# Block-sparse attention and a GELU feed-forward on one core: the first unit's last sampled values moved by SyncE's DMA instead of GpSimd's copies, weights and keys asked for earlier, five more idle products, and new orders for the later units

## The chip, the cores and the metric

The kernel runs on one core of one Trainium2 chip. The metric is the device time in microseconds of one execution; the median of three runs stands for a kernel. PE is TensorE, DVE is VectorE, ACT is ScalarE, POOL is GpSimd and SP is SyncE, as in the profile.

## The reference, cut to what matters

```python
B, H, S, D = 4, 8, 768, 64        # q, k, v in float32
block, n_blocks, n_rand = 32, 24, 3
scores = q @ k^T / sqrt(D)
# a query block sees: itself and its two neighbours, block 0, block 23,
# and its 3 sampled blocks; the query blocks 0 and 23 see everything
attn = softmax(where(mask, scores, -1e9)) @ v
x = attn.transpose(0, 2, 1, 3).reshape(B * S, H * D)      # 3072 x 512
h = x @ w_in                                              # 512 x 2048
out = (0.5 * h * (1 + erf(h / sqrt(2)))) @ w_out          # 2048 x 512
```

The numbers of the sampled blocks are an input, so which blocks are fetched is known only on the device.

## The kernel before

The 24 query blocks of each of the four batches are worked off in two units, so there are eight units in all. The first unit of a batch holds the two query blocks that see everything (the dense rounds, in the plan's letters group d) and three groups a, b and c of block rows, up to four query blocks each; the second holds three groups. Units are numbered from one here; the array `units` counts from 0, and `PLANS[1]` to `PLANS[7]` belong to units two to eight.

Every query block with a window sees eight key blocks. The sampled three are put side by side in the tile `gb`: one copy per block and sampled number, whose source position is a register that holds the block's number (`gather`, line 299). A copy of the keys has 128 columns, one of the values 260, one of both 388. The tiles `kv0` and `kv1` hold keys and values of the even and the odd batches; for the first batch the keys lie in `k0`.

A unit goes through two phases. In its attention phase, scores (line 346), a maximum on DVE (372, 375), exponentials on ACT (389, 393), a transpose on DVE (406, 411), products with the values (433, 470), a division on DVE (485 to 489) and a transpose and copy of the result into `xT` (499, 507, 512) follow one another for every round. PE fills the gaps with FFN2 products of the unit before (`ffn2_pieces`, line 566). Then comes FFN1, 64 products of 128x384 with a GELU behind every two output tiles (523, 545).

The order on every engine is the order of the program: a plan, written as a string of words, is read from left to right. `s3` is the score of round 3, `m3` its maximum, `e3` its exponentials, `t3` its transpose; `wa`, `da`, `oa` are the value products, division and output of group a (`wd0` and `wd1` two halves, `Oc` the output in two parts); `f5` takes five products from the filler; `S` stores finished rows, `G` loads the GELU table; a word that starts with `x` calls a function by name. In the first unit the filler is not FFN2 but `idle_products` (line 572): 128x128 by 128x512 products of the identity matrix, whose result nobody reads. In unit two `xk0`, `xq0` and so on turn the second batch's keys and queries, a pair of heads at a time (`turn_pair`, line 246); a `d` at the end gives the copy behind it to DVE, otherwise ACT makes it.

In the first unit most of the sampled blocks are copied by POOL. Its queue, in order: the loads of the first batch, the first half of `w_in` (lines 666 and 669), the keys of groups b and c, and then, called by the plan as `xv0`, `xv1`, `xv2`, the values of groups a, b and c (`values_of`, line 674). Between them it asks for the last two quarters of `w_in` and, after group c's values, for `w_out` in two halves and the second batch's keys and queries in four transfers (lines 685 to 689). All of these transfers convert from float32 to bf16 and stand in one queue. A group's value products read their sampled values from `gb`:

```python
src = sampled(unit.place[j], c - 4)[:, c0:c0 + V2]
...
work.append((s, 1, c, src))
```

At the end of the first unit the plan reads `... t9 db xn wc ob xa dc xb Oc xc`: `xa`, `xb` and `xc` are FFN1 products of the columns that are ready by then. SP issues one small load at the start and then only the stores of the output, and from the third batch on the transposes by DMA.

The tile `g` (128 x 16 x 384, bf16) takes the GELU's result in FFN1 and is read by FFN2 in the next unit.

Of the kernel before, what the change touches and what calls it, by code (L numbers as in the profile page):

```python
# [20 lines left out]
def kernel(  # L21
# [80 lines left out]
    def sampled(i, r):  # L102
        c0 = GW * (i // 3) + 4 * BW + DW * (i % 3) + BW * r
        return gb[:, c0:c0 + BW]

    def keys(b):
        return kvs[b % 2][:, :, 0:KC]
# [311 lines left out]
    def values(unit, grp, halves):  # L419
# [6 lines left out]
        if grp[0][0] == "d":  # L426
            pv = ptd.rearrange("p g c x q e -> p g c (x q) e")
            for c in range(NB // 2 * halves[0], NB // 2 * (halves[-1] + 1)):
                for G in range(2):
                    for h in range(2):  # L430
                        rows = slice(64 * h, 64 * h + 64)
                        c0 = KC + V2 * G
                        nc.tensor.matmul(av[64 * G:64 * G + 64, h, 0:V2],  # L433
                                         lhsT=pv[rows, G, c // 2, :, c % 2],
                                         rhs=kv[rows, c, c0:c0 + V2],
                                         start=(c == 0), stop=(c == NB - 1))
            n, m = 4, 2
        else:
            slots = [j for rnd in grp for j in rnd[1]]
            pv = st[grp, "pt"].rearrange("p g c (q e) -> p g c q e", e=2)  # L440

            shared = len(slots) == 4
            for G in halves:
                c0 = KC + V2 * G
                ends = [(0, 4, c, kv[:, blk, c0:c0 + V2]) for c, blk in ((0, 0), (7, NB - 1))] if shared else []
                work = []
                for c in range(1, 7) if shared else range(8):
                    for s, j in enumerate(slots):
                        if c in (0, 7):
                            blk = 0 if c == 0 else NB - 1  # L450
                            if abs(blk - j) <= 1:
                                continue
                            src = kv[:, blk, c0:c0 + V2]
                        elif c < 4:
                            src = kv[:, j - 2 + c, c0:c0 + V2]
                        else:
                            src = sampled(unit.place[j], c - 4)[:, c0:c0 + V2]
                        work.append((s, 1, c, src))
                work = work + ends if len(halves) == 2 and G else ends + work
                fresh, left = set(range(len(slots))), {s: 0 for s in range(len(slots))}  # L460
                for s, w, _, _ in work:
                    for x in range(s, s + w):
                        left[x] += 1
                for s, w, c, src in work:
                    at = range(s, s + w)
                    for x in at:
                        left[x] -= 1
                    for h in range(2):
                        rows = slice(64 * h, 64 * h + 64)
                        nc.tensor.matmul(av[32 * s:32 * (s + w), h, V2 * G:V2 * G + V2],  # L470
                                         lhsT=pv[rows, G, c % 4, BL * s:BL * (s + w), c // 4], rhs=src[rows],
                                         start=s in fresh, stop=left[s] == 0)
                    fresh -= set(at)
            n, m = len(slots), 4
            if 1 in halves:
                st.pop((grp, "pt"))
# [95 lines left out]
    def idle_products(m):  # L572

        op = psO.tile([P, D_MODEL], F32, name="op", tag="op")
        for _ in range(m):
            nc.tensor.matmul(op, lhsT=identity, rhs=qT0[:, 0].rearrange("p r s -> p (r s)"),
                             start=True, stop=True)
            yield

    def store_finished():  # L580
# [90 lines left out]
    gather(units[0], grps[2], others, 0, KC, nc.gpsimd)  # L671
    others |= block_numbers(grps[0], POOL)

    def values_of(t):

        def ask():
            js = grps[t]
            if t != 1:
                i = 2 - t // 2
                gather(units[0], js[:i], others, KC, BW, nc.gpsimd)  # L680
                load_w_in(2 + t // 2)
                js = js[i:]
            gather(units[0], js, others, KC, BW, nc.gpsimd)
            if t == 2:
                load_w_out(0, 2)
                load_w_out(1, 2)
                for hs in HALVES:
# [5 lines left out]
    def more_numbers(js):  # L693
        def load():
            for c in range(0, len(js), 6):
                known.update(block_numbers(js[c:c + 6], DVE))
        return load
    attention(units[0], idle_products(21),
# [3 lines left out]
              {"f1": lambda: fixed(1), "f2": lambda: fixed(2, nc.scalar.copy, 0),  # L702
               "f3": lambda: fixed(2, nc.scalar.copy, 1), "v0": values_of(0), "v1": values_of(1),
               "v2": values_of(2), "n": more_numbers(J1[:3]),
               "a": lambda: ffn1_ahead(0, (0, 0, P), (0, 1, P)),
               "b": lambda: ffn1_ahead(0, (0, 0, 2 * P)),
               "c": lambda: ffn1_ahead(0, (0, 1, 2 * P), (2, 0, 2 * P), (2, 1, 2 * P))})
# [1 line left out]
    def next_keys(b):  # L709
# [1 line left out]
        spare_key(keys(b))  # L711

    PLANS = {
# [17 lines left out]
    }  # L731

    for n, unit in enumerate(units):
# [83 lines left out]
```

## Time and profile before

| | us |
|---|---|
| median of 3 runs | 273.88 |
| lowest and highest run | 273.58, 276.53 |
| the profiled execution, all of it | 275.15 |
| its span, first to last instruction | 273.4 |
| PE busy in the span | 250.3 |
| mean granted clock of PE | 0.988 |

The span ends 1.75 us short of the profiled execution's time; what lies around it is not in the trace. The page gives, for the whole span, busy time by engine, forty equal slices of 6.8 us (a digit is a tenth), the queues, and groups of instructions by source line. The windows give the same for any stretch, and the timeline gives the instructions of one engine with the idle time before each and what ended it. Ends of PE's products are modelled, and a few records can be missing.

### The profile page before, as it was taken

To read this page: it belongs to the slowest core of one execution; us is meant where nothing else is said; L and a number is where in the kernel's file an instruction comes from. 1 tells how busy PE (TensorE), PEld (TensorE's weight loads), DVE (VectorE), ACT (ScalarE), POOL (GpSimd) and SP (SyncE) were. 2 spreads that over 40 slices of the span, in tenths; PEclk is the share of its full clock that TensorE was granted. 3 is DMA by queue.
4 is the path that set the end of the run, shared out by engine and by line. 5 is a ranking of instruction groups with operands and counts; after the bars stand their busy time and mean duration, and the time that the engine had idled before them with its cause. 6 is when DMAs were issued, how large, how long until landed. Compare 5 with 4: busy or idle time off the path is not lost.

```text
span 273.4 us, 11478 instructions
## 1 busy us (share of the span) xinstructions
PE 250.3 (92%) x4899; PEld 143.7 (53%) x4933; DVE 208.3 (76%) x477; ACT 206.7 (76%) x378; POOL 101.7 (37%) x210
## 2 busy tenths in 40 slices
PE   0798699899999999999999999999999999999995
PEld 0624486355564555545555566455645655465544
DVE  7599969598898989589998987698949996882000
ACT  8679766896868885797868976988788966985611
POOL 7797980717595000950962003910040033000000
PEclk9999689999999999999999999999999999999999
DMA  6999499959999317991997108991101110111002
GB/s 96 183 70 163 75 148 193 206 116 122 63 161 142 102 43 112 114 88 42 120 152 119 62 35 154 89 61 44 40 0 43 43 41 0 38 44 43 0 38 77
DMA packets 73508, 23.80 MB, mean 87 GB/s; under 512 B 63089, under 2 KB 70514, under 8 KB 73458
## 3 DMA queue, kind: packets, MB, share of 16 engines
q0 software_dynamic: 57440, 13.64, 84.4%
q1 hardware_dynamic: 16018, 9.44, 13.6%
q8 instruction: 38, 0.62, 1.0%
q14 instruction: 12, 0.10, 0.1%
HBM read 27.26 MB, written 6.29 MB: 123 GB/s over the span
## 4 chain that ended last, share of the span: by engine, by line
PE 73%; DMA 9%; ACT 6%; DVE 5%; issue 3%; POOL 3%; POOLq 0%; ACTq 0%
PE hp L523 27%; PE op L566 22%; PE av L470 9%; PE sc L346 6%; DMA kn<-in_k_dram 6%; DMA qn<-in_q_dram 3%; PE tx L499 2%; PE op L596 2%; ACT L417 2%; PE pt L234 2%; PE av L433 2%; ACT pp L393 2%; PE av L596 1%; POOL gb L304 1%; ACT pp L389 1%
## 5 line engine op out<-in xcount | busy, mean ns | idle before, releaser
L523 PE MATMUL hp<-xT,w_in_sb 128*128 128x384 bf16 (+2 forms) x536 | 84.9, 319 | 0.2 <-ACT xT L507 0.2
L389 ACT ACTIVATE pp<-sc,nm 128x256 bf16<-128x256 f32 x176 | 74.9, 540 | 7.7 <-DVE nm L372 7.1
L566 PE MATMUL op<-w_out_sb,g 128*128 128x512 bf16 x305 | 75.8, 380 | 4.0 <-issue 3.8
L523 PEld LDWEIGHTS <-w_in_sb 128*128 128x128 bf16 x536 | 51.1, 98 | 33.1 <-issue 0.3
L545 ACT ACTIVATE g<-hp 128x768 bf16<-128x768 f32 x56 | 45.2, 809 | 25.9 <-PE hp L523 25.9
L372 DVE TENSOR_REDUCE nm<-sc 128x4 f32<-128x1024 f32 (+1 forms) x48 | 53.2, 1115 | 6.3 <-PE sc L346 6.0
L566 PEld LDWEIGHTS <-g 128*128 128x128 bf16 x336 | 28.7, 98 | 34.0 <-issue 6.5
L304 POOL COPY gb<-kv 128x388 bf16 (+1 forms) x87 | 36.6, 472 | 23.8 <-DVE gb L295 21.6
L304 DVE COPY gb<-kv 128x388 bf16 x177 | 38.4, 295 | 0.3 <-DVE gb L295 0.2
L406 DVE STREAM_TRANSPOSE pT<-pp 128x512 f32<-128x512 f32 (+1 forms) x48 | 31.4, 657 | 5.3 <-ACT pp L389 4.6
L470 PE MATMUL av<-kv,pT 64*32 64x130 bf16 (+1 forms) x1344 | 30.6, 229 | 1.9 <-DVE pT L406 1.2
L470 PEld LDWEIGHTS <-pT 64*32 64x32 bf16 (+1 forms) x2400 | 26.2, 94 | 10.2 <-DVE pT L406 4.0
L165 POOL COPY mark<-gb 1x1 bf16<-1x1 bf16 x6 | 1.1, 178 | 76.5 <-DVE gb L304 76.5
L141 POOL DMA_DIRECT2D kv<-in_v_dram x32 | 23.0, 726 | 2.5 <-DMA qn<-in_q_dram 1.4
L346 PE MATMUL sc<-gb,qT 64*32 64x256 bf16 x704 | 18.5, 275 | 2.6 <-ACT pp L389 1.8
L507 ACT COPY xT<-tx 128x512 bf16<-128x512 bf16 (+1 forms) x32 | 13.7, 453 | 9.1 <-PE tx L499 9.1
L470 PE MATMUL av<-gb,pT 64*32 64x130 bf16 x1056 | 20.2, 231 | 0.0
L346 PEld LDWEIGHTS <-qT 64*32 64x32 bf16 x832 | 9.3, 90 | 20.4 <-issue 12.3
L417 ACT ACT_TABLE_LOAD x15 | 19.2, 1283 | 0.2
L489 DVE TENSOR_TENSOR xh<-av,rec 128x512 bf16<-128x512 f32 (+2 forms) x28 | 18.2, 652 | 1.0
L393 ACT ACTIVATE pp<-sc,nm 128x768 bf16<-128x768 f32 x16 | 16.7, 1101 | 2.5 <-DVE nm L375 2.2
L550 ACT COPY os<-op 128x512 f32<-128x512 f32 (+1 forms) x23 | 13.1, 570 | 7.0 <-PE op L596 4.3
(79 smaller groups left out, 230.2 us busy)
## 6 DMA issues: line engine op xcount, KB each, us to landing
out_dram<-os SPq DMA_DIRECT2D x23, 256.0 KB, 3.3
kv<-in_v_dram POOLq DMA_DIRECT2D x32, 96.0 KB, 6.6
w_in_sb<-in_moe_w_in_dram POOLq DMA_DIRECT2D x4, 512.0 KB, 7.3
w_out_sb<-in_moe_w_out_dram POOLq DMA_DIRECT2D x2, 1024.0 KB, 12.1
kn<-in_k_dram POOLq DMA_DIRECT2D x4, 384.0 KB, 10.8
qn<-in_q_dram POOLq DMA_DIRECT2D x4, 384.0 KB, 12.2
qn<-in_q_dram POOLq DMA_DIRECT2D x12, 128.0 KB, 5.4
kn<-in_k_dram POOLq DMA_DIRECT2D x12, 128.0 KB, 5.9
```

Source lines behind the costliest of these rows:

```text
L141: nc.gpsimd.dma_start(out=kvs[b % 2][32 * hh:32 * hh + 32, 0:NB, c0:c0 + D], in_=v[b, h].rearrange("(n p) d -> p n d", p=BL))
L304: (engine or nc.vector).tensor_copy(sampled(unit.place[j], r)[:, None, c0:c1], src[:, bass.ds(at[j][r], 1), :])
L346: nc.tensor.matmul(o, lhsT=qT[rows, j // 4, pr, BL * (j % 4):BL * (j % 4) + BL], rhs=rhs(rows, pr), start=True, stop=True)
L372: nc.vector.tensor_reduce(out=nm[:, 0:2 * n].rearrange("p (g j) -> p g j", g=2), in_=A4[:, :, 0:n, :], op=ALU.max, axis=AX.X, negate=True)
L389: nc.scalar.activation(at[:, x // n, x % n], A[:, a:a + 256].rearrange("p (e c k) -> p e c k", e=2, k=BL), AF.Exp, bias=nm[:, x:x + 1])
L393: nc.scalar.activation(pp[:, 0:S].rearrange("p (c k e) -> p c e k", e=2, k=BL), A[:, 0:S].rearrange("p (c e k) -> p c e k", e=2, k=BL), AF ...
L406: nc.vector.transpose(pt.rearrange("p g c x -> p (g c) x")[:, :, 64 * s:64 * (s + n)].bitcast(F32), pp[:, 0:512 * n].bitcast(F32).rearrang ...
L417: nc.scalar.activation(junk, zero[0:1, 0:1], func)
L470: nc.tensor.matmul(av[32 * s:32 * (s + w), h, V2 * G:V2 * G + V2], lhsT=pv[rows, G, c % 4, BL * s:BL * (s + w), c // 4], rhs=src[rows], st ...
L523: nc.tensor.matmul(hp[:, i, c0:c1], lhsT=w_in_sb[:, ki, (m + i) * P:(m + i + 1) * P], rhs=xTs[n % 2][:, ki, c0:c1], start=(ki == 0), stop= ...
L545: nc.scalar.activation(g[:, m:m + 2, 0:T], hp[:, :, 0:T], AF.Gelu)
L566: nc.tensor.matmul(op, lhsT=g[:, m, t * P:(t + 1) * P], rhs=w_out_sb[:, m, :], start=(m == 0), stop=(m == KOUT - 1))
```

## The change

The three sampled value blocks of each of group c's three query blocks (nine blocks of 128 x 260) are no longer copied into `gb` by POOL. They go by nine DMAs, issued by SP with the block number in a register of SP, into the tail of the tile `g`, which nothing has written yet in the first unit (`early`). A memset of one element by POOL stands ahead of the first DMA, so that SP waits until POOL has come to that place, behind the copies of two of group a's blocks and the third quarter of `w_in`. Group c's value products read from there.

POOL then copies only the values of groups a and b. The last quarter of `w_in` is asked for after the first block of group b, and `w_out` and the second batch's keys and queries after group b.

The first four idle products are made in two halves of 256 columns, and there are 26 instead of 21; the added ones stand as `f1` before `wd0`, before `wd1` and before `wa`, and as `f2` before `od`. The call `xv2` is gone.

The plans of units two to eight are replaced. In unit two the first key turn `xk0d` stands after three filler products (`f3`) instead of twelve, and the copies of some turns change engine. In units three to eight, scores, divisions and filler products change places within the engines' orders; their number does not change.

```diff
+    early = g.rearrange("p m t -> p (m t)")[:, KOUT * UT - 3 * NR * 2 * V2:].rearrange("p (x c) -> p x c", c=2 * V2)
+
+    def sampled_values(unit, j, r):
+        if unit is units[0] and j in unit.groups[-1]:
+            return early[:, NR * unit.groups[-1].index(j) + r]
+        return sampled(unit.place[j], r)[:, KC:BW]
...
-                            src = sampled(unit.place[j], c - 4)[:, c0:c0 + V2]
+                            src = sampled_values(unit, j, c - 4)[:, c0 - KC:c0 - KC + V2]
...
-        for _ in range(m):
-            nc.tensor.matmul(op, lhsT=identity, rhs=qT0[:, 0].rearrange("p r s -> p (r s)"),
-                             start=True, stop=True)
+        row = qT0[:, 0].rearrange("p r s -> p (r s)")
+        for i in range(m):
+            w = D_MODEL // (2 if i < 4 else 1)
+            for c0 in range(0, D_MODEL, w):
+                nc.tensor.matmul(op[:, c0:c0 + w], lhsT=identity, rhs=row[:, c0:c0 + w], start=True, stop=True)
             yield
...
+    late_numbers = block_numbers(grps[2], mybir.EngineType.SP)
+
+    def fetch_values():
+
+        nc.gpsimd.memset(early[0:1, 0, 0:1], 0.0)
+        for j in grps[2]:
+            for r in range(NR):
+                nc.sync.dma_start(out=sampled_values(units[0], j, r)[:, None, :],
+                                  in_=kvs[0][:, bass.ds(late_numbers[j][r], 1), KC:BW])
+
     def values_of(t):
 
         def ask():
-            js = grps[t]
-            if t != 1:
-                i = 2 - t // 2
-                gather(units[0], js[:i], others, KC, BW, nc.gpsimd)
-                load_w_in(2 + t // 2)
-                js = js[i:]
-            gather(units[0], js, others, KC, BW, nc.gpsimd)
-            if t == 2:
+            i = 2 - t
+            gather(units[0], grps[t][:i], others, KC, BW, nc.gpsimd)
+            load_w_in(2 + t)
+            if t == 0:
+                fetch_values()
+            gather(units[0], grps[t][i:], others, KC, BW, nc.gpsimd)
+            if t == 1:
                 load_w_out(0, 2)
                 load_w_out(1, 2)
...
-    attention(units[0], idle_products(21),
+    attention(units[0], idle_products(26),
               "s0 m0 s1 m1 e0 xf1 f3 s2 t0 m2 e1 xf2 f1 s3 t1 m3 e2 f8 s4 t2 m4 e3 xf3 f3 s5 t3 m5 e4 xv0 f6 "
-              "s6 t4 m6 e5 wd0 s7 t5 m7 e6 xv1 wd1 s8 dd t6 m8 e7 wa s9 da t7 m9 e8 xv2 od wb "
+              "s6 t4 m6 e5 f1 wd0 s7 t5 m7 e6 xv1 f1 wd1 s8 dd t6 m8 e7 f1 wa s9 da t7 m9 e8 f2 od wb "
               "t8 e9 G oa t9 db xn wc ob xa dc xb Oc xc",
...
     PLANS = {
-        1: ("s0 m0 s1 f12 m1 e0 e1 S xk0d s2 f1 m2 t0 f5 s3 e2 xq0d f5 m3 t1 xk1 t2 e3 s4 m4 f4 xq1 xv wa  "
-            "s5 t3 m5 xk2d f5 e4 s6 f1 da e5 xq2 wb m6 t5 db S xq3 t4 s7 f3 m7 oa f3 xk3d wc f1 e7 e6 ob  "
-            "f4 dc t7 Oc t6 f5 xs G"),
-        2: ("S s1 s0 m1 f3 e1 f6 m0 s2 t1 m2 e0 e2 t0 f7 s3 wd s4 m3 f2 t2 f4 e3 dd m4 od e4 f4 t3 s5 m5  "
-            "wa e5 s6 t4 m6 f6 da f2 s7 m7 e6 e7 S f1 t5 G f5 t6 oa t7 wb wc db f1 dc ob f4 Oc"),
...
+        1: ("s0 s1 m0 e0 f3 m1 xk0d f8 e1 s2 xq0 S f5 s3 m2 t0 f4 t1 e2 xk1d wa xq1 xv s4 t2 m3 f6 e3 f1  "
+            "xk2 m4 f5 da s5 t3 m5 xq2d wb e4 f1 S e5 xq3 s6 t4 f3 db m6 oa f2 s7 t5 e6 m7 xk3 t6 wc e7  "
+            "dc f2 ob t7 f4 Oc G f5 xs"),
+        2: ("s1 f2 s0 f1 m1 e1 m0 f6 t1 s2 e0 f5 m2 e2 t0 f1 s3 wd m3 e3 t2 s4 f4 m4 f2 s5 dd m5 e4 e5 f7  "
+            "s6 f1 od t3 m6 wa t4 s7 e6 f10 da m7 e7 t5 S oa wb t6 t7 db wc f1 dc S ob f4 Oc G f1"),
...
```

More of the change, by code (lines that the diff above doesn't have):

```diff
@@ L703 @@
                "f3": lambda: fixed(2, nc.scalar.copy, 1), "v0": values_of(0), "v1": values_of(1),
-               "v2": values_of(2), "n": more_numbers(J1[:3]),
+               "n": more_numbers(J1[:3]),
                "a": lambda: ffn1_ahead(0, (0, 0, P), (0, 1, P)),
```

22 rows, old and new, of the table PLANS are left out of this document.

## The prediction

> **What bounds the kernel now.** I read the page first, then the stretches of the first unit by window, then the order of events on each engine there, then the transfers.
>
> ```profile
> span 273.4 us, 11478 instructions
> PE 250.3 (92%) x4899; PEld 143.7 (53%) x4933; DVE 208.3 (76%) x477; ACT 206.7 (76%) x378; POOL 101.7 (37%) x210
> PEclk9999689999999999999999999999999999999999
> ```
>
> TensorE (PE) is the bound, and almost nothing of its work is removed. A gain can come only from its idle time or from the one place where its clock is low. How much idle time lies where:
>
> ```profile
> 48.44:72.40 23.96, 21.96 (x590) 12.43 (x595) 19.52 (x31) 19.01 (x39) 12.01 (x29) 1.00 1.70 132
> sum 114.14, PE 108.78 PEld 59.61 DVE 98.33 ACT 99.28 POOL 21.19; mean PE 18.13 PEld 9.93 DVE 16.39 ACT 16.55 POOL 3.53
> ```
>
> The columns are start:end, length, then busy time of each engine. The second unit's attention leaves PE idle for 2.0 us. The sum is over the attention stretches of units three to eight, 5.36 us idle in all. The other unit work is dense. What the edits to the code can win lies before 53 us.
>
> ```profile
> 22.80:26.20 3.40, 2.64 (x85) 1.36 (x70) 2.96 (x5) 3.40 (x10) 3.23 (x9) 1.00 1.11 187
> 26.20:29.60 3.40, 1.96 (x100) 1.23 (x107) 3.33 (x7) 3.03 (x8) 3.40 (x11) 0.99 1.00 146
> 29.60:36.35 6.75, 5.57 (x254) 3.89 (x255) 5.57 (x12) 5.23 (x13) 6.75 (x19) 0.50 0.33 47
> 30.00:33.80 3.80, 2.62 (x118) 1.53 (x106) 3.31 (x7) 2.31 (x8) 3.80 (x11) 0.50 0.02 5
> 46.00:50.90 4.90, 4.85 (x55) 2.43 (x55) 3.98 (x15) 4.29 (x8) 2.61 (x7) 1.00 1.24 206
> ```
>
> The last three columns are granted clock, DMA share and GB/s. After a stretch in which PE was busy for only 58% the clock falls to 0.50 for 6.75 us; the stretch before, with 78%, kept it. And from 30.0 to 33.8 us the DMA engines move 5 GB/s, while later they are full at 206.
>
> ```profile
> 26.53 0.41 PE L346 MATMUL sc<-gb,qT 64*32 64x256 bf16 x16 [0.36 <-ACT pp L389]
> 28.62 0.41 PE L346 MATMUL sc<-gb,qT 64*32 64x256 bf16 x16 [0.87 <-ACT pp L389]
> 29.27 0.75 PE L470 MATMUL av<-kv,pT 64*128 64x130 bf16 x28 [0.24 <-DVE xh L489]
> 33.17 0.85 PE L470 MATMUL av<-kv,pT 64*128 64x130 bf16 x28 [1.18 <-DVE pT L406]
> 35.80 0.62 PE L470 MATMUL av<-kv,pT 64*32 64x130 bf16 x22
> 36.12 0.51 PE L470 MATMUL av<-gb,pT 64*32 64x130 bf16 x18
> 48.44 0.63 PE L346 MATMUL sc<-gb,qT 64*32 64x256 bf16 x32
> 52.86 0.53 PE L234 MATMUL pt<-identity,kn 96*64 96x96 bf16 x16 [0.93 <-DMA kn<-in_k_dram]
> ```
>
> This is the timeline of PE: start, length, operation, and in brackets the idle time before it with its cause. The first unit's three value products start at 29.27 (group a), 33.17 (b) and 35.8 (c; its products with sampled values from 36.12). PE then runs FFN1 without a gap, and stands 0.93 us for the next batch's keys.
>
> **The change part by part.** First GpSimd (POOL):
>
> ```profile
> 25.05 0.74 POOL L154 DMA_DIRECT2D w_in_sb<-in_moe_w_in_dram  x1
> 25.78 7.31 POOL L304 COPY gb<-kv 128x260 bf16 x21
> 33.04 0.74 POOL L154 DMA_DIRECT2D w_in_sb<-in_moe_w_in_dram  x1
> 33.78 2.12 POOL L304 COPY gb<-kv 128x260 bf16 x6
> 35.85 1.76 POOL L159 DMA_DIRECT2D w_out_sb<-in_moe_w_out_dram  x2
> 37.59 0.70 POOL L110 DMA_DIRECT2D kn<-in_k_dram  x1
> ```
>
> A copy takes 2.12/6 = 0.353 us. Nine go, 3.2 us; one memset of a single element comes, some 0.2 us by estimate (the copies are its nearest row). So the last w_in part, which stood behind 27 copies and now stands behind 15, is asked for 12 x 0.353 - 0.2 = 4.0 us sooner, at 29.0. The two w_out halves and the keys and queries are asked for 3.0 us sooner, the keys at 34.6. No engine waits at POOL in this time, so the copies themselves cost the end nothing until group c's values, of which the last copy ends at 35.9, 0.2 us ahead of their use at 36.12.
>
> The nine transfers on SyncE (SP) begin after that memset, at 25.9. SP has nothing else queued until a store at 55.35, so its register loads and its waits hold nobody up. The trace shows no transfer of 128 rows of 520 bytes (67 KB). Its nearest rows are the stores:
>
> ```profile
> out_dram<-os SPq DMA_DIRECT2D x2, 128.0 KB, 1.7
> 55.35 0.38 SPq L552 DMA_DIRECT2D out_dram<-os  x1
> out_dram<-os SPq DMA_DIRECT2D x1, 256.0 KB, 4.0
> ```
>
> The last column of the first and third is us to landing, the third beside full loads. Nine issues of 0.38 us, with 0.1 each for the address by estimate, end at 30.2, and the last lands 1.7 to 4.0 later, at 32 to 34. Group c needs them from 36.1 now and 35.2 with a full clock (below). One after another, at 1.7 each, they would land at 25.9 + 15.3 = 41.2: the other bound. I take 33, since SP does not wait for one store before it issues the next at the end of the kernel, and the row with the smaller transfer is the nearer. So they cost nothing.
>
> The five idle products take about 0.22 us each (a product of the same 512 columns, below, 0.21). One goes before each half of the dense round's value products, one before group a's, two before od. The gaps of 0.36, 0.87, 0.24 and 1.18 us in the rows above hide them; without these gaps they would cost 1.1. Two of them, and 0.2 us of work pushed over the border by the first, raise the stretch 26.2 to 29.6 from 1.96 to 2.6 us busy of 3.4, 76%: just under what kept the clock. The first four products split in two have the same columns and cost nothing by that measure; if each extra start cost 0.05 it would be 0.2, ahead of scores with slack. I take the clock to hold, 6 in 10.
>
> What that is worth:
>
> ```profile
> 92.91 1.38 PE av L470 x104
> 29.76 1.19 DVE L372 TENSOR_REDUCE nm<-sc 128x4 f32<-128x1024 f32 x1
> 31.37 0.17 DVE L485 TENSOR_SCALAR den<-av 128x8 f32<-128x8 f32 x1 [0.42 <-PE av L470]
> 34.77 0.45 DVE L406 STREAM_TRANSPOSE pT<-pp 128x256 f32<-128x256 f32 x1 [0.47 <-ACT pp L389]
> 35.38 0.17 DVE L485 TENSOR_SCALAR den<-av 128x8 f32<-128x8 f32 x1 [0.15 <-PE av L470]
> 35.81 0.69 DVE L489 TENSOR_TENSOR xh<-av,rec 128x512 bf16<-128x512 f32 x1
> 37.20 0.17 DVE L485 TENSOR_SCALAR den<-av 96x8 f32<-96x8 f32 x1 [0.70 <-PE av L470]
> 33.79 0.95 ACT L389 ACTIVATE pp<-sc,nm 128x256 bf16<-128x256 f32 x2 [0.76 <-DVE nm L372]
> 100.39 1.04 PE av L470 x86
> ```
>
> At full clock group a's products take 1.38 instead of the 2.1 us up to 31.37 and end at 30.7, so VectorE (DVE) divides right after its reduce ends at 30.95: 0.42 sooner. The next reduce, the last exponentials (33.79) and the last transpose (34.77) follow 0.42 sooner, the transpose ending at 34.8. Group b is done by 34.2, so its division starts at 34.95 and, taking 1.1 us as it did from 35.38 to 35.81 + 0.69, ends about 36.1. Group c runs 34.85 to 35.9 (1.04 at full clock) and needs its sampled values at 35.2: GpSimd's last copy at 35.9 would have held it 0.7, and this is what their move buys. Its division starts at 36.1 instead of 37.20: FFN1 and all DVE work behind it come 1.1 sooner, and PE reaches the next unit's scores at 47.3 instead of 48.44.
>
> What is late next is the keys. Their transfer and the queue of nine products:
>
> ```profile
> 37.59 15.22 DMA kn<-in_k_dram
> 114.78 2.97 PE op L566 x13
> ```
>
> The keys took 15.2 us because they stand behind w_in and w_out in a full queue. Asked for 3.0 sooner they land at 52.8 - 3.0 = 49.8. The bounds: 48.8 if w_in's 4.0 decides, 52.7 if SP's 9 x 67 KB = 0.6 MB at 206 GB/s, 2.9 us, stands in the way. I take 49.8: the order of the requests is kept and the 0.6 MB, in flight from 26 to 33, falls mostly on the 3.8 us in which the engines moved nothing. [...]
>
> Unit two's new order asks PE for the key turn after 3 instead of 12 FFN2 products. One takes 2.97/14 = 0.21 us (fourteen stand in the order, thirteen are recorded). PE arrives at 47.3 + 0.63 + 3 x 0.21 + about 0.2 of issue = 48.8 and waits 1.0 us for 49.8. Before, with nine products fewer ahead of it, 52.86 would have been 52.86 - 1.9 = 51.0. Gain 51.0 - 49.8 = 1.2 us. If the clock falls all the same, PE arrives at 49.9 and the gain is 1.1: the keys hide the clock.
>
> The orders of units two to eight also change, mostly by moving a score, a division or some FFN2 products past one another. No row prices that. Its bounds come from the idle time of 2.0 - 0.93 + 5.36 = 6.4 us: it can win a part of it, and lose as much. I take zero.
>
> Sum: 273.4 - 1.2 = 272.2 of span. The profiled execution took 275.15 in all, 1.75 more than its span; the median of the runs shown is 273.88. I put the same gain on the median: **272.7 us**.
>
> **The rivals.** *Keys in time.* They land by 48.8 and the clock holds, so PE does not wait: gain 51.0 - 48.8 = 2.2. If the new orders also close a fifth of the 6.4 us, 1.3, it is 3.5 and 270.4 us. For it: the engines are idle when w_in is now asked for. Against it: w_out, the larger part of the queue, is asked for only 3.0 sooner.
>
> *SP's bytes in the way.* Keys at 52.7, with nine products now behind the turn and not ahead of it: 52.7 - 51.0 = 1.7 lost, 275.6 us. It costs from a landing after 51.0 on. For it: the store beside full loads took 4.0. Against: the hole. [...]
>
> *Values late (slower).* The nine transfers go one after another, and PE stands at group c's sampled products, with FFN1 queued behind them. At 41.2 that is 5.1 after 36.12; the wait for the keys, 0.93, goes in exchange: +4.2, 278.1 us. It decides from (36.1 - 25.9)/9 = 1.13 us per transfer on. [...]
>
> *New orders open waits.* One more wait of 0.6 us (between the 0.24 and the 0.87 of the rows) in each of seven units: 4.2 - 1.2 = +3.0, 276.9 us.
>
> That the idle products fail to hold the clock is the change not doing what it says; it gives 272.8 and is counted with the forecast. [...]
>
> **How the numbers follow.** Forecast 0.48 (own range 271.4 to 274.0), keys in time 0.20, bytes in the way 0.10, values late 0.12, orders 0.10. The range takes in the first three and half of the orders: 269.8 to 276.9. One per cent, 2.7 us, is about what a measurement of this kernel can tell from no change: below 271.1 or above 276.6. Faster: 0.08 of the forecast and 0.19 of the keys, 0.27. Slower: 0.01, 0.02 of the bytes, 0.11 of the values, 0.07 of the orders, 0.21. Within: 0.52.
>
> **What would show it.** SP: nine issues from about 25.9, the last landing by 34. Clock: no 0.50 after 29.6. Group c's division near 36.1. Scores of unit two near 47.3. Key turn near 49.8, with a wait on kn of about 1 us. The forecast is wrong if PE waits at group c's sampled products, if kn lands after 51, or if idle time in units three to eight differs from 5.4 by over 1 us.

## The result and the profile after

| | before | after |
|---|---|---|
| median of 20 runs each, us | 275.28 | 278.61 |
| lowest and highest, us | 273.58, 277.53 | 277.30, 280.73 |
| ratio, 95% interval | | 1.0122 [1.0095, 1.0148] |
| the profiled execution's span, us | 273.4 | 277.6 |

The change makes the kernel 1.2% slower, where 272.7 us were forecast. Of the runs below, a ratio leaves out executions more than 1.5% above the fastest of the same kernel and a median does not, so the two can differ by some tenths of a per cent. The page of the kernel after:

```profile
span 277.6 us, 11561 instructions
PE 257.9 (93%) x4942; PEld 145.8 (53%) x4942; DVE 207.1 (75%) x476; ACT 207.0 (75%) x379; POOL 99.2 (36%) x202
PEclk9999858999999999999999999999999999999999
...
q8 instruction: 38, 0.62, 1.0%
```

The clock digits fall to 5, a slice later than before, where the lowest was 6. The last line is one of the queues, with packets, MB and share of the engines: its 38 packets of 0.62/38 = 0.016 MB are listed as instruction, so no data but program, and their time is given as a share of the same 16 engines, 1.0% of the span.

The timeline of PE in the first unit:

```profile
30.75 0.39 PE L587 MATMUL op<-qT,identity 128*128 128x512 bf16 x1
33.35 0.59 PE L587 MATMUL op<-qT,identity 128*128 128x512 bf16 x1 [2.21 <-issue]
38.45 0.30 PE L478 MATMUL av<-kv,pT 64*32 64x130 bf16 x5 [1.22 <-issue]
38.47 0.61 PE L478 MATMUL av<-g,pT 64*32 64x130 bf16 x18
41.99 10.60 PE L531 MATMUL hp<-xT,w_in_sb 128*128 128x128 bf16 x76
52.52 0.63 PE L354 MATMUL sc<-gb,qT 64*32 64x256 bf16 x32
53.84 0.53 PE L242 MATMUL pt<-identity,kn 96*64 96x96 bf16 x16
```

Two gaps are new, 2.21 us between the two idle products ahead of the dense rounds' output (`od`) and 1.22 us inside group c's products. Both say "issue": PE waited for nothing that the profile shows, no value, no semaphore. The second stands at products with `kv` and not at those with `g`, the tile that SP's transfers write. Unit two's scores begin at 52.52, before at 48.44. The key turn at 53.84 does not wait.

Windows of after, then of before (columns as in the prediction):

```profile
0.00:31.00 31.00, 20.53 (x477) 12.13 (x478) 25.11 (x58) 24.84 (x36) 25.77 (x73) 1.00 1.88 139
0.00:37.20 37.20, 24.52 (x605) 14.47 (x606) 28.98 (x66) 29.27 (x46) 31.66 (x83) 0.94 1.75 146
29.60:32.90 3.30, 1.54 (x84) 0.90 (x70) 3.20 (x6) 2.11 (x6) 3.30 (x10) 1.00 1.04 198
32.90:43.10 10.20, 8.53 (x231) 6.60 (x231) 4.99 (x10) 4.37 (x10) 3.99 (x6) 0.50 1.16 185
52.52:277.60 225.08, 219.30 (x4167) 121.15 (x4166) 168.20 (x377) 170.37 (x323) 66.59 (x117) 1.00 0.82 71
```

```profile
48.44:273.40 224.96, 214.15 (x4135) 121.39 (x4166) 169.29 (x378) 170.21 (x322) 66.63 (x119) 1.00 0.87 77
```

From unit two's scores to the end both take 225 us. So the whole 4.1 us lie ahead of 52.52; what comes behind, the new orders among it, came out even. The 4.1 us divide so: FFN1's long run starts at 41.99 instead of 38.56 (+3.4, the gaps and half clock), and takes 10.53 up to the scores instead of 9.88 (+0.65, its first 1.1 us at half clock). The clock is held in the stage in which it fell before, drops at 32.9 after a stretch in which PE was busy 1.54 of 3.30 us, and stays at 0.50 for 10.2 us instead of 6.75. The clock seems the smaller part of the loss: the two of the 20 executions in which it was at 0.999 or more took 277.30 and 277.74 us, still 2.0 and 2.5 above the median before.

What PE was without is in the first two rows. The first gap opens after 477 + 478 = 955 instructions of PE and PEld, the second after 605 + 606 = 1211: 256 apart. The page has 4942 + 4942 of them on 38 program packets, 260 each. So PE stands where one packet's worth of its program ends. The transfers say where the packet was. The first two lines are from after, in the windows from 30.9 to 32.1 and from 36.0 to 37.1 us, the last two from before, in the windows from 29.8 to 30.8 and from 33.2 to 34.3 us:

```profile
q8 instruction: 1, 0.02, 5.3%
q8 instruction: 1, 0.02, 5.5%
q8 instruction: 1, 0.02, 5.8%
q8 instruction: 1, 0.02, 5.4%
```

One packet takes 5.3% of 16 engines over 1.2 us, 1.0 us of one engine. Narrowing the windows puts it at 30.99 to 32.01 and at 36.05 to 37.03 after, and at 29.81 to 30.73 and 33.26 to 34.22 before. Between 32.1 and 36.0 there is none. PE goes on 1.3 to 1.4 us after each end, at 33.35 and 38.45. In the kernel before the packets came 1.2 and 2.8 us earlier, the second in the hole in which 5 GB/s were moved. The longest wait of PE at issue in that whole kernel, by its view of waits (in total, times, longest), is

```profile
PE av L470 <- issue: 0.5, 1, 0.5
```

and the timeline has it at 100 us. After, half of SP's nine transfers lie in the hole: of their 0.6 MB, 0.30 move between 30.0 and 33.8, beside 0.41 MB of the loads, and 0.20 between 33.8 and 36.3. POOL's and SP's timeline, then the view of the tile `g` (one issue in ns, min, median and max, and the first and last start), then the first keys' transfer:

```profile
28.62 0.74 POOL L162 DMA_DIRECT2D w_in_sb<-in_moe_w_in_dram  x1
34.21 0.70 POOL L118 DMA_DIRECT2D kn<-in_k_dram  x1
25.58 6.80 SPq L691 DMA_DIRECT2D g<-kv  x9
```

```profile
L691 SPq DMA_DIRECT2D g<-kv x9: 500/506/1326, 25.6 to 31.1; - x9
DMA to landing us min/median/max: 4.9/5.3/6.0
```

```profile
kn<-in_k_dram POOLq DMA_DIRECT2D x1, 384.0 KB, 15.9
```

POOL is where the prediction put it. SP issues from 25.6 to 32.4. Its queue moves its first data at 29.3 and its last at 36.4.

### The profile page after: what moved, and what is told of

The parts are those of the page before. It is cut to its first block, busy times and chain, and to the rows that moved or that the text cites. A ratio compares the mean times of both kernels' runs of the same rounds, so it can differ in the third digit from the quotient of the medians.

```text
span 277.6 us, 11561 instructions
## 1 busy us (share of the span) xinstructions
PE 257.9 (93%) x4942; PEld 145.8 (53%) x4942; DVE 207.1 (75%) x476; ACT 207.0 (75%) x379; POOL 99.2 (36%) x202
## 4 chain that ended last, share of the span: by engine, by line
PE 83%; ACT 6%; DVE 4%; issue 3%; DMA 3%; POOL 1%; POOLq 0%; ACTq 0%
PE hp L531 30%; PE op L574 25%; PE av L478 12%; PE sc L354 6%; DMA qn<-in_q_dram 3%; PE tx L507 2%; PE op L606 2%; PE av L441 2%; PE pt L242 2%; ACT pp L401 1%; ACT L425 1%; DVE nm L380 1%; ACT pp L397 1%; PE av L606 1%; DVE nm L383 1%
## 5 line engine op out<-in xcount | busy, mean ns | idle before, releaser
L531 PE MATMUL hp<-xT,w_in_sb 128*128 128x384 bf16 (+2 forms) x536 | 86.0, 322 | 0.0
L574 PE MATMUL op<-w_out_sb,g 128*128 128x512 bf16 x336 | 83.8, 381 | 0.7 <-issue 0.5
L531 PEld LDWEIGHTS <-w_in_sb 128*128 128x128 bf16 x536 | 52.1, 100 | 33.0 <-issue 0.2
L312 POOL COPY gb<-kv 128x388 bf16 (+1 forms) x78 | 33.5, 485 | 23.3 <-DVE gb L303 20.8
L383 DVE TENSOR_REDUCE nm<-sc 128x1 f32<-128x768 f32 x16 | 14.8, 948 | 6.2 <-PE sc L354 6.1
L478 PE MATMUL av<-gb,pT 64*32 64x130 bf16 x1020 | 18.9, 226 | 0.0
```

The lines of the kernel that those rows point to most:

```text
L312: (engine or nc.vector).tensor_copy(sampled(unit.place[j], r)[:, None, c0:c1], src[:, bass.ds(at[j][r], 1), :])
L531: nc.tensor.matmul(hp[:, i, c0:c1], lhsT=w_in_sb[:, ki, (m + i) * P:(m + i + 1) * P], rhs=xTs[n % 2][:, ki, c0:c1], start=(ki == 0), stop= ...
L574: nc.tensor.matmul(op, lhsT=g[:, m, t * P:(t + 1) * P], rhs=w_out_sb[:, m, :], start=(m == 0), stop=(m == KOUT - 1))
```

## The experiments

Ratios are to the kernel before on the same chip. The changed kernel itself was not run again beside them, so its 1.0122 is from other executions. Each diff is against the kernel after, unless another is named. The first four take the change apart. Either the added PE instructions open the gaps, or SP's transfers do, by their bytes or by landing late, or the loss hangs on the new orders.

**Without the added idle products.**

```diff
-    attention(units[0], idle_products(26),
+    attention(units[0], idle_products(21),
...
-              "s6 t4 m6 e5 f1 wd0 s7 t5 m7 e6 xv1 f1 wd1 s8 dd t6 m8 e7 f1 wa s9 da t7 m9 e8 f2 od wb "
+              "s6 t4 m6 e5 wd0 s7 t5 m7 e6 xv1 wd1 s8 dd t6 m8 e7 wa s9 da t7 m9 e8 od wb "
```

> The changed kernel without the five added idle products; everything else stays. Code theory (PE stands where the next 256 instructions of its program have not come: the gaps at 30.8 to 33.4 and 36.9 to 38.5 end 1.3 and 1.4 us after a 16 KB packet of the instruction queue): without the products the clock falls near 29.6 as before, PE gets to the border later and the gaps shrink; unit two's scores begin at 48.5 to 50 instead of 52.5, the time is 274 to 276. Values theory (PE stands for the nine transfers from SP, the last of which is moving until 36.4): the gap in group c's products stays, its division is no earlier than 39, unit two's scores at 51 or later and the time 277 or more.

281.22 us, 1.0172 [1.011, 1.0234]. Its timeline of PE:

```profile
33.65 0.53 PE L478 MATMUL av<-kv,pT 64*128 64x130 bf16 x26 [1.48 <-issue]
40.67 0.52 PE L478 MATMUL av<-g,pT 64*32 64x130 bf16 x18 [4.30 <-issue]
```

The first gap has shrunk from 2.21 to 1.48, the second has grown from 1.22 to 4.30, and its packet is at 38.24 to 39.21. Unit two's scores come at 54.41. The products are not the cause. By the numbers written down, this run went as the values theory said and not as the code theory said; which of the two holds, the run in which nobody reads the transfers decides below.

**Only the idle products**, against before:

```diff
-    attention(units[0], idle_products(21),
+    attention(units[0], idle_products(26),
...
-              "s6 t4 m6 e5 wd0 s7 t5 m7 e6 xv1 wd1 s8 dd t6 m8 e7 wa s9 da t7 m9 e8 xv2 od wb "
+              "s6 t4 m6 e5 f1 wd0 s7 t5 m7 e6 xv1 f1 wd1 s8 dd t6 m8 e7 f1 wa s9 da t7 m9 e8 xv2 f2 od wb "
```

> The kernel before with the five added idle products alone, at the same places. Code theory: the clock holds past 29.6, PE gets to the border of its program early and stands there for 1 us or more with nothing else that could hold it (GpSimd still copies the values, SP is idle); the scores of unit two come no sooner than 48.4, up to 50.5; time 274 to 278. Values theory: the products alone hold the clock and nothing stands, scores at 47.3 to 48.2 (group c then waits for GpSimd's last copy), time 273 to 275.

275.53 us, 1.0016 [0.9985, 1.0046]. The longest gap at issue before 68 us is 0.48, where the code theory had asked for 1 us or more. Its timeline:

```profile
47.42 0.63 PE L346 MATMUL sc<-gb,qT 64*32 64x256 bf16 x32
50.23 1.02 PE L566 MATMUL op<-w_out_sb,g 128*128 128x512 bf16 x4 [0.35 <-DMA w_out_sb<-in_moe_w_out_dram]
52.20 0.53 PE L234 MATMUL pt<-identity,kn 96*64 96x96 bf16 x16 [0.94 <-DMA kn<-in_k_dram]
```

The clock is full, the scores come 1.0 earlier than in before's profiled execution, and waits for `w_out` and the keys take 0.35 and 0.94 of it back.

**Group c's values copied by POOL again**, `w_out` and the keys behind them; the last quarter of `w_in` is still asked for sooner, and SP moves nothing:

```diff
...
-            if t == 0:
-                fetch_values()
-            gather(units[0], grps[t][i:], others, KC, BW, nc.gpsimd)
-            if t == 1:
+            if t == 2:
+                gather(units[0], grps[2], others, KC, BW, nc.gpsimd)
...
```

> The changed kernel with group c's values copied by GpSimd again (w_out and the keys then asked for behind them, w_in still sooner), so no transfer from SP in the first unit. Values theory: no gap in group c's products beyond GpSimd's last copy near 35.9, scores of unit two at 48 or sooner, time about 273. Code theory: both gaps at the borders of 256 instructions stay, though each may be up to 1 us shorter where the packets of the instruction queue start sooner without SP's bytes; scores at 50 to 52, time 275 to 278.

279.79 us, 1.021 [1.0147, 1.0273], as slow as the change, by another way:

```profile
31.68 0.38 PE L585 MATMUL op<-qT,identity 128*128 128x512 bf16 x1 [1.21 <-issue]
35.41 0.24 PE L476 MATMUL av<-kv,pT 64*32 64x130 bf16 x5 [0.81 <-issue]
47.62 0.63 PE L352 MATMUL sc<-gb,qT 64*32 64x256 bf16 x32
52.20 0.53 PE L240 MATMUL pt<-identity,kn 96*64 96x96 bf16 x16 [3.20 <-DMA kn<-in_k_dram]
```

Without SP's transfers the two gaps fall to 1.21 and 0.81 and the first unit is as early as in the last experiment. What it loses, it loses later: the new order of unit two turns the keys after three filler products, and keys that are asked for no sooner (at 37.09, before at 37.59) make PE stand 3.20. Behind that wait the clock is at 0.68 from 52.2 to 55.6 and at 0.82 up to 59.0. Of the two theories each has a part here: the gaps stay, but the scores are at 47.62.

**The change with the plans of before**:

```diff
     PLANS = {
-        1: ("s0 s1 m0 e0 f3 m1 xk0d f8 e1 s2 xq0 S f5 s3 m2 t0 f4 t1 e2 xk1d wa xq1 xv s4 t2 m3 f6 e3 f1  "
...
+        1: ("s0 m0 s1 f12 m1 e0 e1 S xk0d s2 f1 m2 t0 f5 s3 e2 xq0d f5 m3 t1 xk1 t2 e3 s4 m4 f4 xq1 xv wa  "
...
```

> The changed kernel with the orders of units two to eight from the kernel before. If the loss is in the first unit alone (both theories), the scores of unit two stay at 52.5 and the time stays within 1 us of the changed kernel, 277 to 279.5. If the new orders cost or win something, the time differs by more than 1 us; the idle time of PE in units three to eight (5.4 us before) tells by how much.

281.58 us, 1.0173 [1.0096, 1.0249]. The time is above the 277 to 279.5 that were expected, but the interval takes in the change's 1.0122. The gaps are there (2.73 and 3.52), and unit two starts at 52.91. The loss does not hang on the new orders.

The next four ask what in SP's transfers it is: their landing, their bytes, their number, or `w_in`, which now runs beside them.

**Nobody reads the transfers.** Group c's products read blocks of `kv` at fixed places instead of the sampled ones, so that nothing waits for SP; the nine transfers stay.

```diff
+    if unit is units[0] and j in unit.groups[-1]:
+        src = kv[:, NR * unit.groups[-1].index(j) + c, c0:c0 + V2]
```

> The changed kernel, with the nine transfers as they are, but group c's products read nine other blocks straight from the values tile, so nothing on PE waits for a transfer from SP; the output is not the reference's. Values theory (group c's products wait for the transfers): the second gap, 36.9 to 38.5, goes; scores of unit two at 51 or sooner, time about 277 or less. Traffic theory (the transfers' bytes hold up the packets that bring PE's program): both gaps stay, each ending 1.3 to 1.5 us after a packet of the instruction queue, scores of unit two at 51.5 to 54.5, time 277 to 282.

282.05 us, 1.0214 [1.0129, 1.03]:

```profile
33.06 0.54 PE L589 MATMUL op<-qT,identity 128*128 128x512 bf16 x1 [2.19 <-issue]
41.18 1.60 PE L480 MATMUL av<-kv,pT 64*32 64x130 bf16 x75 [4.38 <-issue]
```

Both gaps stay, the second larger, its packet at 38.95 to 39.93. That PE waits for late values falls.

**The same with eight columns per transfer** instead of 260 (against the last one).

```diff
-    out=sampled_values(units[0], j, r)[:, None, :],
-    in_=kvs[0][:, bass.ds(late_numbers[j][r], 1), KC:BW])
+    out=sampled_values(units[0], j, r)[:, None, 0:8],
+    in_=kvs[0][:, bass.ds(late_numbers[j][r], 1), KC:KC + 8])
```

> As the run before, but each of the nine transfers moves 8 columns instead of 260 (the output is not the reference's). Traffic by bytes: the packets of the instruction queue start within 1.5 us of the border again, the first gap shrinks from 2.6 to about 1.2 us, the second from 1.5 or more to 1 or less, as in the run in which GpSimd copied the values; scores of unit two near 47.6, a wait for the keys of about 1 us behind them, time 273 to 275.5. Traffic by count (each transfer, however small, holds up the packets): no change, scores at 51.5 or later, time 277 or more.

276.78 us, 1.0016 [0.9975, 1.0057]:

```profile
32.25 0.38 PE L589 MATMUL op<-qT,identity 128*128 128x512 bf16 x1 [1.01 <-issue]
35.98 0.92 PE L480 MATMUL av<-kv,pT 64*32 64x130 bf16 x75 [0.93 <-issue]
42.17 7.25 PE L533 MATMUL hp<-xT,w_in_sb 128*128 128x384 bf16 x43 [0.90 <-issue]
49.35 0.63 PE L354 MATMUL sc<-gb,qT 64*32 64x256 bf16 x32
50.69 0.53 PE L242 MATMUL pt<-identity,kn 96*64 96x96 bf16 x16
```

The same nine issues, waits and places; only the bytes are gone. The packets come at 29.84 and 33.76, nearly as before, the gaps are 1.0 and 0.9, and the intervals of the two ratios, 1.0016 here and 1.0214 with the bytes, do not meet. Here the bytes delay the program. The scores (49.35) and the time are later than the 47.6 and the 273 to 275.5 written down for this: gaps of 0.9 to 1.0 are left, and one of 2.07 at 69.77. So without the bytes the change, as far as this run shows it, would be no faster than before, though PE turns the keys at 50.69 without a wait.

**The last quarter of w_in later**, behind group b's copies, so that it no longer runs beside SP's transfers:

```diff
-            i = 2 - t
+            i = 2 if t == 0 else 4
```

> The changed kernel with the last quarter of w_in asked for behind all of group b's copies, at about 31.8 instead of 28.6, so that SP's nine transfers have the engines nearly to themselves from 30 to 33. If the overlap of SP's transfers with that load holds up the program: first gap 1.5 us or less, scores of unit two at 48 to 50, time 274 to 276. If SP's transfers do it by themselves: gaps as in the changed kernel, scores at 51.5 or later, time 277 or more.

281.33 us, 1.0213 [1.0142, 1.0284], gaps of 2.43 and 4.89 us. For the first gap SP's transfers do it without `w_in` beside them: from 30.2 to 31.2 they move 0.31 MB, the loads 0.01, and the packet starts at 31.18. By the second, `w_in` and `w_out` are under way again.

**The border moved.** If PE stands where its program runs out, 128 more instructions ahead of it must move the gap by 128, to other work. Sixty-four products of 32x32 with zeros, made at the start while PE is idle:

```diff
...
+    for _ in range(64):
+        nc.tensor.matmul(pad[0:32, 0:32], lhsT=blank, rhs=blank, start=True, stop=True)
```

> The changed kernel with 64 tiny products of a zero tile (128 instructions) in PE's idle time at the start, so that every border of 256 instructions falls 128 instructions sooner in the work. [...] If the gaps belong to the operations and not to the program's borders: they stay at the same operations, 2.6 us at the idle products and 1.5 us in group c's products.

298.35 us (293.87 to 300.76 in four runs) against 276.12, the median of 13. Its timeline of PE, and its windows up to the start of each gap:

```profile
33.33 0.29 PE L483 MATMUL av<-gb,pT 64*32 64x130 bf16 x3 [2.91 <-issue]
39.80 0.42 PE L483 MATMUL av<-kv,pT 64*32 64x130 bf16 x15 [1.98 <-issue]
45.73 0.30 PE L483 MATMUL av<-g,pT 64*32 64x130 bf16 x5 [2.68 <-issue]
```

```profile
0.00:30.60 30.60, 21.61 (x477) 13.08 (x478) 24.02 (x57) 24.48 (x35) 24.99 (x70) 1.00 1.99 131
0.00:38.00 38.00, 25.79 (x605) 15.36 (x606) 27.58 (x63) 27.59 (x43) 31.93 (x83) 0.92 1.81 142
0.00:43.00 43.00, 28.98 (x733) 17.73 (x734) 29.08 (x67) 29.67 (x46) 31.93 (x83) 0.87 1.73 145
```

The gaps stand at other work, all inside value products, and at the same counts, 955 and 1211, with the next border, 1467, added. The page has 39 program packets instead of 38. That PE stands at borders of its program is shown. The price was not foreseen: six more gaps of over 1.1 us each, the last at 267 us.

The rest looked for a faster version and for what the border costs alone.

**Keys between the quarters of w_out**, with the idle products of the second experiment and before's plans; then the **same requests without the products**:

```diff
-    load_w_out(0, 2)
-    load_w_out(1, 2)
-    for hs in HALVES:
-        load_kq(kn, k, hs, 1)
-        load_kq(qn, q, hs, 1)
+    for part in range(3):
+        load_w_out(part)
+    load_kq(kn, k, HALVES[0], 1)
+    load_w_out(3)
+    load_kq(qn, q, HALVES[0], 1)
+    load_kq(kn, k, HALVES[1], 1)
+    load_kq(qn, q, HALVES[1], 1)
```

> The kernel before with the five idle products and with w_out asked for in quarters, the first half of the second batch's keys between the third and the fourth (queries behind it, then the second halves); no transfer from SP, old orders of units two to eight. If the keys hide what the held clock wins (FFN1 1.0 us sooner, then 0.9 us of wait for the keys and 0.4 for w_out in the run with the idle products alone): scores of unit two near 47.4, no wait over 0.3 us at the key turn, time 1.0 to 1.5 us below the kernel before, ratio 0.994 to 0.998. If the keys are not what hides it: ratio 0.999 to 1.004.

> The kernel before with the new order of the requests alone, no added idle products. Scores of unit two stay near 48.4, the wait of 0.93 us for the keys goes: ratio 0.996 to 0.999. If the wait only hides other ones behind it: ratio 1.0.

275.05 us, 0.9986 [0.9956, 1.0016], and 274.80 us, 0.9995 [0.9968, 1.0021]. The keys' wait is gone in both, PE turning them at 51.79 and 50.83, and neither is measurably faster; for the first 0.994 to 0.998 were expected. Its scores come at 48.53 instead of 47.4, behind a gap of 0.88 at 36.36, again after 1211 instructions. The second has a full clock without any added product, and one row that the prediction had worked out:

```profile
35.06 0.72 PE L470 MATMUL av<-gb,pT 64*32 64x130 bf16 x14 [0.74 <-POOL gb L304]
```

**The kernel before with the 64 tiny products**; then **twelve**, 24 instructions, in the kernel with the keys between, in the one before and in the one after:

```diff
...
+    for _ in range(12):
+        nc.tensor.matmul(pad[0:32, 0:32], lhsT=blank, rhs=blank, start=True, stop=True)
```

> The kernel before with the 64 tiny products (128 instructions) in PE's idle time at its start and nothing else. Code theory: the borders of 256 instructions fall inside the value products of the groups here too, so gaps open there and the time rises by 3 to 15 us although the added work is hidden. If the borders matter only beside SP's transfers: time within 1 us of the kernel before.

> The kernel before with the five idle products and the new order of requests, plus 12 tiny products (24 instructions) in PE's idle time at the start, so that every border of 256 instructions falls 24 instructions sooner. In the traces the gaps left in the later units come where PE runs through two groups' products before a border; 24 instructions sooner, most of the borders lie where PE was slower on the way. Code theory: the gaps over 0.4 us behind 60 us (2.5 us in all without the shift) fall to 1 us or less, ratio to the kernel before 0.990 to 0.996. If the remaining gaps are not set by the borders: ratio 0.997 to 1.002.

> The kernel before with the 12 tiny products alone. Code theory: its gaps (0.7 at 99.7, 0.6 at 68.0, and more in other runs of it) fall or go, ratio 0.993 to 0.999; nowhere near the rise that 64 tiny products gave. If any shift costs: ratio 1.01 or more.

> The changed kernel with the 12 tiny products. If the borders alone set the loss: the two gaps of the first unit fall under 1 us each and the ratio to the kernel before is 1.00 or less. If the late packet beside SP's transfers sets it: the gaps of the first unit stay at 3.5 us or more together, 24 instructions sooner in the program, and the ratio stays at 1.008 or above.

Sixty-four cost the kernel before 14 to 21 us (289.02 to 295.74 in four runs, against 274.86, the median of 23), at the top of the 3 to 15 that were expected, or above it. Twelve were to put the borders at better places, and a gain was expected. The kernel before went to 278.68 us, 1.0159 [1.0115, 1.0204], the one with the keys between to 279.63, 1.0184 [1.0138, 1.0231]: missed. The window of the former from unit two's scores to the end:

```profile
48.02:276.60 228.58, 214.48 (x4135) 121.04 (x4166) 169.29 (x378) 170.56 (x321) 66.82 (x118) 1.00 0.84 76
```

The first unit is 0.4 sooner than before, and the loss of 3.6 us comes behind it, at the same busy time of PE (214.48 for 214.15). With the change, 286.68 us, 1.0413 [1.0358, 1.0468], the first unit loses too, as the second of the two branches written down for it has it; its timeline shows gaps at borders that have moved:

```profile
33.89 0.27 PE L483 MATMUL av<-kv,pT 64*128 64x130 bf16 x3 [3.21 <-issue]
40.63 0.52 PE L483 MATMUL av<-kv,pT 64*32 64x130 bf16 x17 [1.70 <-issue]
```

That the place of the borders costs per cents is measured. Which place is good is not understood: the one forecast made for it failed twice, and this stays open. The rows give a part of it. With GpSimd's copies and with eight columns, PE goes on at two borders in a row 3.73 us apart (31.68 and 35.41, 32.25 and 35.98): the packet starts 1.5 to 1.6 us behind the first, moves for 1.0, and PE goes on 1.2 to 1.3 later. By estimate from these rows, a stretch of 256 instructions that PE runs through in less than 3.7 us ends in a gap even without SP's bytes; with them the packet started 2.7 us behind the first border (33.35 to 36.05), and 5.9 where nobody reads (33.06 to 38.95). This was not tried as a rule for placing borders.

## Why the prediction was wrong

**The step that failed.** "So they cost nothing", said of the nine transfers, with "the 0.6 MB, in flight from 26 to 33, falls mostly on the 3.8 us in which the engines moved nothing". Of the bytes, half fell there: the transfers moved from 29.3 to 36.4, not from 26 to 33. But the hole was in use: at its edge and in it, from 29.81 and from 33.26, went two packets of PE's program. The prediction's own row showed the second, as its 5 GB/s. These are the transfers of before from 30.0 to 33.8 by queue:

```profile
q8 instruction: 1, 0.02, 1.6%
q0 software_dynamic: 6, 0.00, 0.3%
```

One packet of 0.016 MB in 3.8 us is 4.3 GB/s. With SP's bytes on the engines the two packets start at 30.99 and 36.05, PE stands 2.21 and 1.22 us, and the clock falls within the first gap. Nine transfers that nobody reads gave 1.0214 whole and 1.0016 as eight columns each. The gain in the sum, 1.2 us at the keys, went with it: the keys landed as forecast, but PE came to them at 53.84 and not at 48.8.

**SP's bytes in the way**, the rival at 0.10, had the traffic right and the victim wrong. The keys were asked for at 34.21 and landed 15.9 later, at 50.1, where 49.8 was forecast; PE was not there until 53.84. What was held up is the program: where nobody reads, its second packet started at 38.95 with SP's transfers whole and at 33.76 with eight columns each.

**Values late**, at 0.12, gave the nearest time, 278.1, for a reason that is not so. The term was mis-sized: an issue takes 0.5 us and one comes every (31.1 - 25.6)/8 = 0.69 and not 0.48, a transfer lands 4.9 to 6.0 us after its issue and not 1.7 to 4.0, and the last data move at 36.4 and not 33. The 0.1 for an address was the author's estimate, without a row; so was the 0.2 of issue ahead of the key turn, where scores to turn took 53.84 - 52.52 = 1.32 us and not 0.63 + 3 x 0.21 + 0.2 = 1.46. But PE's gaps stay when nobody reads the values.

**The clock** was weighed on one execution. Before's profiled one, at 0.988, lies among the few: of 60 further executions of it, 43 had a mean clock of 0.997 or more and four below 0.99. So the 0.50 from 29.6 on, and what the products should win by ending it, were mostly not there to be won. That the products cost nothing is right (1.0016 with them alone), and all ten runs with them were at 0.998 or more, as were ten of 13 of the kernel before on that chip. The changed kernel is at 0.997 or more in two of 20 executions and below 0.99 in 11: there the lower clock is the common case.

**Right**: POOL's requests (28.62 and 34.21, forecast 29.0 and 34.6), SP's start (25.58 for 25.9), the scores at full clock (47.42 for 47.3), and that the keys hide this gain (0.94 of 1.0). POOL's last copy does hold group c at full clock, 0.74 where 0.7 was worked out; that is the most that the move could save in this unit, against 4.1 lost. That the scores agree is in part luck: 47.3 counted on the move, and the run with 47.42 lacks it. The new orders are near the zero that was taken: 225.1 against 225.0 from the scores on, with the keys' wait of 0.93 gone and one of 0.85 at issue new at 71.72, another border by its count: 1242 + 1242 = 2484 records of PE stand ahead of it, and six packets behind 955 would be 2491, of which a few can be missing. In the run with the new requests alone, 1245 + 1246 = 2491 stand ahead of its gap at 67.78. Their key turn after three products, though, hangs on the earlier request and costs 3.2 us without it.

**The idle time of units three to eight**, by which the new orders were bounded, was largely not idle. The sum over the same six stretches of after, from a unit's first scores to its FFN1, and the FFN2 products of before and after on their pages:

```profile
sum 114.75, PE 113.09 PEld 59.44 DVE 97.20 ACT 96.37 POOL 21.91; mean PE 18.85 PEld 9.91 DVE 16.20 ACT 16.06 POOL 3.65
L566 PE MATMUL op<-w_out_sb,g 128*128 128x512 bf16 x305 | 75.8, 380 | 4.0 <-issue 3.8
L574 PE MATMUL op<-w_out_sb,g 128*128 128x512 bf16 x336 | 83.8, 381 | 0.7 <-issue 0.5
```

The idle time is 1.66 us and not 5.36, though the stretches are no shorter. The record of before lacks 31 of the 336 products, and their time appears there as 24 waits at issue of up to 0.2 us, 3.8 in all. So the sign that was set for these units, a difference of over 1 us, came for a reason that is not the change, and most of the 6.4 us was never there to be won.

## What to carry to other kernels

In the stretch in which the DMA engines of this kernel moved 5 GB/s, and at its edge, two packets of PE's program went, from 29.81 and 33.26: look at the instruction queue's packets before filling such a stretch, and at what PE has left to run. The gaps at "issue" that recurred here at fixed counts of PE's instructions, 955 and 1211, were borders of its program, and 128 instructions added ahead of them moved them to other work. A stage priced from one profiled execution, such as a clock that falls, should first be counted over the other runs: here 43 of 60 had a mean clock of 0.997 or more.

## What the runs showed of the hardware

PE's program came in packets of 0.016 MB, 38 on the page of the kernel after and 39 with 128 instructions more, and PE stood after 955, 1211 and 1467 instructions, 256 apart. Where it stood in the first unit a packet took about 1.0 us and PE went on 1.2 to 1.6 us after its end. It stood 0.8 to 1.2 us at a border there without SP's bytes (GpSimd's copies, eight columns), and up to 4.9 us when the packet was late beside SP's 0.6 MB and the loads (the last quarter of `w_in` later). Sixty-four tiny products, made where PE stood for the first keys anyway (6.48 us in the kernel before), cost the kernel before at least 14 us (289.02 against 274.86).

Nine transfers of 65 KB between places in SBUF, issued by SP beside a load, were 4.9 to 6.0 us under way each in the kernel after.

In the kernel after, the clock fell to 0.50 after a window of 3.3 us in which PE was busy for 47%, and came back after 10.2 us.
